# The second pass of a 192-row matmul as two 64-row tiles of the TensorE array

## Chip, cores, metric

The kernel runs on one core of one Trainium2 chip. The metric is the device time of a whole execution in microseconds (us). Ratios are the mean time of one kernel's fast runs over that of the other's of the same rounds, with a 95% interval; so they are not quite the ratio of the medians quoted beside them.

## The reference

```python
# x: (8, 4096, 192), weight_gen: (8, 4096, 8 heads, 7 taps)
w = softmax(weight_gen, axis=-1)
out = einsum('bshk,bskhg->bshg', w, windows_of_7_rows(x))   # dynamic convolution
h = out.reshape(32768, 192) @ w_in                          # 192 -> 2048
result = (h - tanh(h)) @ w_out                              # 2048 -> 192
```

## The kernel before

It works on 64 blocks of 512 tokens. POOL multiplies the seven shifted copies of x by the softmax weights (`prod`), DVE adds them in pairs (`gsum`), and PE transposes and sums the groups against an identity into `pc`. ScalarE (ACT) evicts `pc` into `convT` (input rows 0 to 127) and `convT1` (rows 128 to 191). Then PE makes `ph` = w_in x conv for two 128-wide f tiles at a time, ACT takes tanh (`th`), DVE subtracts (`gt`), and PE makes the output `po`. `pc`, `ph` and `po` lie in PSUM, where the kernel keeps the outputs of matmuls; to evict is to copy out of it. In the profiles, PEld is the loading of a matmul's weights.

192 input rows do not fill two passes of 128. The kernel before fills up with zeros: the columns 192 to 255 of each `gsum`, and the rows 64 to 127 of `w_in1`.

```python
    w_in1 = const.tile([P, F], BF16, name="w_in1")
    nc.vector.memzero(w_in1[D1:P, :])                            # D1 = 64, P = 128
    nc.gpsimd.dma_start(out=w_in1[0:D1, :], in_=moe_w_in[D0:D, :])
    # ... in the sums of a block:
                nc.gpsimd.memzero(acc[:, :, D:DP])               # L179: D = 192, DP = 256
    # ... in the first matmul; fa and fb are the two f tiles, ph has one PSUM bank for each:
            # L227 and L234: ph[a], ph[b] = w_in0 x convT        (128 rows)
            nc.tensor.matmul(ph[:, 0:TOK],                       # L241
                lhsT=w_in1[:, fa * P : (fa + 1) * P], rhs=convT1[:], start=False, stop=True)
            nc.tensor.matmul(ph[:, TOK : 2 * TOK],               # L248
                lhsT=w_in1[:, fb * P : (fb + 1) * P], rhs=convT1[:], start=False, stop=True)
    # ... (cut: loads, softmax, transposes L194 to L206, evictions, output L272 and L279)
```

The steps of transposing (`gen_phase_a2`), first matmul (`gen_phase_b`) and output matmul (`gen_phase_c`) of neighbouring blocks are interleaved in the program, and the compiler then orders the instructions of each engine.

The softmax here doesn't subtract the row's maximum and nothing guards it: scores larger than these inputs give would overflow.

## Time and profile before

1045.23 us, median of two runs. The table is from the windows view over eight blocks of the long stage (436.4 to 552.8 us) and from the busy table.

| engine | us busy per block | share of the whole span |
|---|---|---|
| PE | 14.2 | 89% |
| DVE | 11.8 | 77% |
| POOL | 11.4 | 71% |
| ACT | 10.3 | 64% |

The lines themselves, and how they are read, stand in the prediction. In short: a head of about 16 blocks, in which POOL and DVE lead, then 48 blocks in which PE sets the pace. A plain one of them takes 14.27 us. I split every run below at the end of block 15's last `gt`: the head is what comes before it, and the long stage is from there to block 63's last `gt`. Before, they took 341.4 and 691.9 us of a span of 1041.2, with 7.9 us of tail.

### The profile page before, as it was taken

The page shows a single profiled execution, that of the slowest core. Times are in us where ns is not written, and L with a number is a line of the kernel's source. Part 1 is how long each engine was busy: PE and PEld are TensorE (multiplying, and loading weights), DVE is VectorE, ACT ScalarE, POOL GpSimd, SP SyncE. Part 2 cuts the span into 40 slices and gives each one's busy share as a digit, 9 for nine tenths or more (in the row PEclk, how much of TensorE's full clock was granted, in tenths as well). Part 3 has the DMA queues.
Part 4 walks back from the last instruction along what each step waited for, and adds up shares of the span by engine and source line. Part 5 has one row for each costly group of instructions (what it writes and reads, how often), then busy time and mean ns, then how long its engine had stood idle before and what let it go on. Part 6 is the DMA issues. An engine that isn't in the chain of part 4 may idle for free.

```text
span 1041.2 us, 20956 instructions
## 1 busy us (share of the span) xinstructions
PE 931.3 (89%) x8192; PEld 661.6 (64%) x8192; DVE 803.0 (77%) x945; ACT 665.2 (64%) x961; POOL 739.3 (71%) x713
## 2 busy tenths in 40 slices
PE   0576777798999999999999999999999999999998
PEld 0344554465666777667776777667776777777776
DVE  1587777797887888788887888788887888877665
ACT  0254445465666777767776777677776777777775
POOL 4868868898786778867787778867787777882000
PEclk9999899899999999999999999999999999999999
DMA  8947588687997787777776777777876777510001
GB/s 167 314 132 230 169 242 250 202 264 223 331 289 208 236 242 222 220 214 235 238 219 205 236 237 233 216 211 231 243 223 202 235 227 239 153 62 27 21 31 47
DMA packets 306579, 211.48 MB, mean 203 GB/s; under 512 B 44312, under 2 KB 306288, under 8 KB 306480
## 3 DMA queue, kind: packets, MB, share of 16 engines
q1 hardware_dynamic: 304192, 208.58, 67.4%
q0 software_dynamic: 2288, 1.57, 1.1%
q8 instruction: 64, 1.05, 0.4%
q14 instruction: 35, 0.29, 0.1%
HBM read 186.52 MB, written 25.17 MB: 203 GB/s over the span
## 4 chain that ended last, share of the span: by engine, by line
PE 55%; POOL 17%; DVE 9%; issue 5%; ACT 5%; SPq 4%; DMA 3%; POOLq 0%; ACTq 0%; DVEq 0%
POOL prod L155 17%; PE po L272 10%; PE po L279 10%; PE ph L248 8%; PE ph L227 7%; PE ph L234 7%; PE ph L241 7%; DVE gt L258 5%; PE pc L194 2%; DVE gsum L174 2%; DMA wg_t<-in_weight_gen_dram 2%; SPq L123 2%; PE pc L206 2%; PE pc L198 2%; PE pc L202 2%
## 5 line engine op out<-in xcount | busy, mean ns | idle before, releaser
L155 POOL TENSOR_TENSOR prod<-xs,wsm 128x768 bf16<-128x768 f32 x448 | 687.1, 1563 | 100.1 <-DVE wsm L146 45.5
L256 ACT ACTIVATE th<-ph 128x1024 f32<-128x1024 f32 x512 | 519.1, 1023 | 283.9 <-PE ph L248 270.9
L258 DVE TENSOR_TENSOR gt<-ph,th 128x1024 bf16<-128x1024 f32 x512 | 609.9, 1210 | 83.0 <-ACT th L256 82.4
L272 PE MATMUL po<-w_out_t,gt 128*128 128x192 bf16 x2048 | 383.4, 248 | 2.1 <-ACT out_sb L288 2.1
L279 PE MATMUL po<-w_out_t,gt 128*128 128x192 bf16 x2048 | 383.1, 248 | 0.0
L227 PE MATMUL ph<-convT,w_in 128*128 128x512 bf16 x512 | 196.6, 384 | 57.0 <-DVE gt L258 55.5
L279 PEld LDWEIGHTS <-gt 128*128 128x128 bf16 x2048 | 201.8, 99 | 27.2 <-issue 4.8
L272 PEld LDWEIGHTS <-gt 128*128 128x128 bf16 x2048 | 201.9, 99 | 24.7 <-issue 1.3
L248 PE MATMUL ph<-convT,w_in 128*128 128x512 bf16 x512 | 197.1, 385 | 0.0
L241 PE MATMUL ph<-convT,w_in 128*128 128x512 bf16 x512 | 196.8, 384 | 0.0
L234 PE MATMUL ph<-convT,w_in 128*128 128x512 bf16 x512 | 196.6, 384 | 0.0
L174 DVE TENSOR_TENSOR gsum<-prod,prod 128x768 bf16<-128x768 bf16 x192 | 137.1, 759 | 41.1 <-POOL prod L155 41.1
L179 POOL MEMSET gsum<- 128x128 uint32 x192 | 38.6, 204 | 127.9 <-DVE gsum L174 126.5
L194 PE MATMUL pc<-ident,gsum 128*128 128x128 bf16 x384 | 84.9, 221 | 42.9 <-DVE gsum L174 32.1
L234 PEld LDWEIGHTS <-w_in 128*128 128x128 bf16 x512 | 50.4, 98 | 66.0 <-issue 65.8
L241 PEld LDWEIGHTS <-w_in 128*128 128x128 bf16 x512 | 50.5, 99 | 62.0 <-issue 3.0
L198 PE MATMUL pc<-ident,gsum 128*128 128x128 bf16 x384 | 84.9, 221 | 4.0 <-POOL gsum L179 3.9
L206 PE MATMUL pc<-ident,gsum 128*128 128x128 bf16 x384 | 85.1, 222 | 0.0
L248 PEld LDWEIGHTS <-w_in 128*128 128x128 bf16 x512 | 50.5, 99 | 54.4 <-issue 2.2
L202 PE MATMUL pc<-ident,gsum 128*128 128x128 bf16 x384 | 85.1, 222 | 0.0
L194 PEld LDWEIGHTS <-gsum 128*128 128x128 bf16 x384 | 38.0, 99 | 55.8 <-DVE gsum L174 33.2
L198 PEld LDWEIGHTS <-gsum 128*128 128x128 bf16 x384 | 37.8, 98 | 54.2 <-issue 26.3
(31 smaller groups left out, 579.6 us busy)
## 6 DMA issues: line engine op xcount, KB each, us to landing
xs<-in_x_dram SPq DMA_DIRECT2D x400, 384.0 KB
out_dram<-out_sb SPq DMA_DIRECT2D x64, 384.0 KB
xs<-in_x_dram SPq DMA_DIRECT2D x48, 288.0 KB
wg_t<-in_weight_gen_dram SPq DMA_DIRECT2D x64, 112.0 KB
w_out_t<-in_moe_w_out_dram POOLq DMA_DIRECT2D x1, 768.0 KB, 17.0
xs<-in_x_dram SPq DMA_DIRECT2D x8, 95.2 KB
xs<-in_x_dram SPq DMA_DIRECT2D x8, 94.5 KB
xs<-in_x_dram SPq DMA_DIRECT2D x8, 93.8 KB
```

What stands on the lines that cost most here:

```text
L155: nc.gpsimd.tensor_mul(prod[:, :, 0:D].rearrange("p j (h g) -> p j h g", h=H), xs[k][:].rearrange("p j (h g) -> p j h g", h=H), wsm[:, :, ...
L174: nc.vector.tensor_add(acc[:, :, 0:D], prods[taps[0]][:, :, 0:D], prods[taps[1]][:, :, 0:D])
L194: nc.tensor.matmul(pc[:, 0:P], lhsT=gsums[g][:, j0, 0:D0], rhs=ident[:], start=st0, stop=False,)
L198: nc.tensor.matmul(pc[:, P : 2 * P], lhsT=gsums[g][:, j1, 0:D0], rhs=ident[:], start=False, stop=False,)
L227: nc.tensor.matmul(ph[:, 0:TOK], lhsT=w_in0[:, fa * P : (fa + 1) * P], rhs=convT[:], start=True, stop=False,)
L234: nc.tensor.matmul(ph[:, TOK : 2 * TOK], lhsT=w_in0[:, fb * P : (fb + 1) * P], rhs=convT[:], start=True, stop=False,)
L241: nc.tensor.matmul(ph[:, 0:TOK], lhsT=w_in1[:, fa * P : (fa + 1) * P], rhs=convT1[:], start=False, stop=True,)
L248: nc.tensor.matmul(ph[:, TOK : 2 * TOK], lhsT=w_in1[:, fb * P : (fb + 1) * P], rhs=convT1[:], start=False, stop=True,)
L256: nc.scalar.activation(out=th[:], in_=ph[:], func=ACT.Tanh)
L258: nc.vector.tensor_sub(gt[:], ph[:], th[:])
L272: nc.tensor.matmul(po[:, 0:D], lhsT=gts[ft // 2][:, gto + j0 * P : gto + (j0 + 1) * P], rhs=w_out_t[:, ft, :], start=(ft == 0), stop=False,)
L279: nc.tensor.matmul(po[:, D : 2 * D], lhsT=gts[ft // 2][:, gto + j1 * P : gto + (j1 + 1) * P], rhs=w_out_t[:, ft, :], start=False, stop=(ft ...
```

## The change

It gives the second pass the 64 rows that it needs and is meant to run the passes of fa and fb at once, as two tiles: fa in rows 0 to 63 of the array, fb in rows 64 to 127. Going from full-array matmuls to these tiles, or back, is called a change of mode, or a switch, below. For that both halves of `w_in1` hold the same weights, and the last 64 columns of each `gsum` are copied behind themselves, so that `convT1` comes out with its 64 rows twice.

```diff
-    nc.vector.memzero(w_in1[D1:P, :])
     nc.gpsimd.dma_start(out=w_in1[0:D1, :], in_=moe_w_in[D0:D, :])
+    nc.gpsimd.dma_start(out=w_in1[D1:P, :], in_=moe_w_in[D0:D, :])
@@
-                nc.gpsimd.memzero(acc[:, :, D:DP])
+                nc.gpsimd.tensor_copy(acc[:, :, D:DP], acc[:, :, D0:D])
@@
-                lhsT=w_in1[:, fa * P : (fa + 1) * P],
-                rhs=convT1[:],
+                lhsT=w_in1[0:D1, fa * P : (fa + 1) * P],
+                rhs=convT1[0:D1, :],
@@
-                lhsT=w_in1[:, fb * P : (fb + 1) * P],
-                rhs=convT1[:],
+                lhsT=w_in1[D1:P, fb * P : (fb + 1) * P],
+                rhs=convT1[D1:P, :],
```

## The prediction

> **What bounds the kernel now.** I read the page first: the busy table, the 40 slices, the chain, the groups.
>
> ```profile
> PE 931.3 (89%) x8192; PEld 661.6 (64%) x8192; DVE 803.0 (77%) x945; ACT 665.2 (64%) x961; POOL 739.3 (71%) x713
> ...
> PE   0576777798999999999999999999999999999998
> ...
> PE 55%; POOL 17%; DVE 9%; issue 5%; ACT 5%; SPq 4%; DMA 3%; POOLq 0%; ACTq 0%; DVEq 0%
> ...
> L179 POOL MEMSET gsum<- 128x128 uint32 x192 | 38.6, 204 | 127.9 <-DVE gsum L174 126.5
> ```
>
> PE is at 9 tenths in all slices from the tenth on and at 5 to 8 before. So there are two stages: a head of some 290 us in which the chain runs through POOL's products and DVE's sums, and a long stage in which PE never stops. The memset row matters later: POOL already waits for DVE's gsum there.
>
> Next, the windows view over one stretch of the long stage, and the timeline of PE in it.
>
> ```profile
> 436.40:552.80 116.40, 113.75 (x1028) 81.65 (x1026) 94.30 (x118) 82.75 (x121) 91.21 (x89) 1.00 0.76 225
> ```
>
> ```profile
> 703.16 0.38 PE L227 MATMUL ph<-convT,w_in 128*128 128x512 bf16 x1
> 703.38 0.38 PE L234 MATMUL ph<-convT,w_in 128*128 128x512 bf16 x1
> 703.59 0.38 PE L241 MATMUL ph<-convT,w_in 128*128 128x512 bf16 x1
> 703.81 0.38 PE L248 MATMUL ph<-convT,w_in 128*128 128x512 bf16 x1
> 704.02 0.22 PE L194 MATMUL pc<-ident,gsum 128*128 128x128 bf16 x1
> 704.08 0.22 PE L198 MATMUL pc<-ident,gsum 128*128 128x128 bf16 x1
> ```
>
> The window holds 8 of the 64 blocks of 512 tokens: 14.55 us a block, of which PE is busy in 98%; DVE needs 94.30/8 = 11.8, POOL 11.4, ACT 10.3, and the DMA share 0.76 means some 11.1 at full use. The matmul records overlap, so I use the step from start to start: 0.216 us for a 512-column matmul (703.38 to 703.59), 0.055 for a 128-column one, and 0.0825 for a 192-column one (elsewhere in the same timeline). One block has 32, 32 and 64 of them: 6.91 + 1.78 + 5.28 = 13.97 us. That is nearly the whole period, so PE's start-to-start stream sets the long stage.
>
> One detail bears on the change. In time order, L241 is followed directly by L248 450 times out of 512; 61 times, about once a block, conversion matmuls stand between them:
>
> ```profile
> 707.31 0.38 PE L241 MATMUL ph<-convT,w_in 128*128 128x512 bf16 x1
> 707.82 0.22 PE L194 MATMUL pc<-ident,gsum 128*128 128x128 bf16 x1
> ...
> 708.04 0.38 PE L248 MATMUL ph<-convT,w_in 128*128 128x512 bf16 x1
> ```
>
> Such a pair cannot run side by side if the order stays as it is.
>
> **What the Trainium skill says.** "TensorE: Matmul & The Clock Gate", Part 3, says that tiles of different row groups run together, starting about 4 ns apart, and that a weight load overlaps a running matmul in that way only when the row group differs. "TensorEngine Tiling (Array Packing)", Key Properties: "Changing tiling mode (not just tile) drains the TensorE"; it gives no size for this. Its restrictions say that different row tiles must write to different PSUM banks; ph holds 2 x 512 fp32, and the halves go to the two tiles. "GPSIMD Engine Reference", section 4.1, calls one-input operations there roughly line-rate. The trace before agrees as far as it can: its 512-column step is 216 ns; but every record is a 128*128 operation, so neither the concurrency nor the drain is seen in it.
>
> **The change part by part.**
> *Removed.* Per pair of f tiles, two 216 ns passes become one. If the order stays, 450 pairs gain: 450 x 0.216 = 97 us of PE time; the 62 split ones gain nothing. The memset of w_in1 (one instruction, 0.9 us at the start) goes.
> *Added, PE.* Each pair is now a stretch in another tiling mode between full-array work: two switches, and four for a split pair, 450 x 2 + 62 x 4 = 1148 switches. Each costs an unknown s. Its bounds from the trace, as estimates: a matmul's record is 384 ns against a 216 ns step, so 168 ns lie between the end of streaming and the recorded end; and where a weight load and its matmul had both been waiting, the matmul starts 53 ns after the load at the least. If a switch waits for the whole record and then exposes the load, s is 168 + 53 = 221 ns. If only the array empties while reads go ahead, s is perhaps a third of the 168, with the load hidden: 56 ns. If it is overlapped, 0. Break-even is 97 / 1148 = 85 ns.
> I choose 60 ns as the middle: 1148 x 0.060 = 69 us added, 28 us net off PE.
> *Added, POOL.* 256 memsets of 204 ns become copies of 256 bf16 elements per partition. Near line rate with some dispatch I estimate 350 to 450 ns, so 256 x 0.2 = 50 us more busy time, 739 to some 790. In the long stage POOL has 14.55 - 11.4 = 3.1 us of slack a block and needs 0.8 of it: hidden. In the head POOL is on the chain: some 20 blocks' worth of products run there, but only two or so copies a block stand between one product and the next that the chain needs, so 20 x 2 x 0.2 = 8 us on the path. The wait for gsum is no new one.
> *Added, DMA.* w_in1's upper half is loaded a second time in the first tens of microseconds; the first matmul that needs it starts at about 38 us. Nothing.
> *Sum.* 51 to 52 of 64 blocks are in the long stage, so 0.8 of a change in PE's work reaches the end: 0.8 x (-28) = -23 us. With +8 of the head: -15. 1045 - 15 = 1030 us.
>
> **Rivals.**
> (a) The full drain. With s = 221, PE gains 97 and pays 254: +157, times 0.85 is +133, and 8 of the head, some 1185 us. For it: the page's bare word "drains", and the design before, which zero-pads 64 rows to 128 and pays 51 us of POOL memsets for that, as one would to stay in one mode. Against it: that padding also pays with a much smaller s.
> (b) A switch that costs almost nothing. PE's block falls from 14.3 to 12.8 us. Then the loop between POOL and DVE takes over: in one block POOL runs six products in a row (9.04 us), waits for DVE's sums, runs the four fills (now 0.4 each), the seventh product (1.54), and DVE's wsm (0.39) precedes the next. That is 9.04 + 0.8 + 1.6 + 1.54 + 0.39, with some 0.3 of handovers, 13.7 at worst with all fills on the path, 12.6 with one. So the gain ends near 1 us a block: 51 x 1.0 = 51 off, 8 back: about 1000 us. For it: the reported concurrency. Against it: the modes alternate 16 times a block, not in long runs.
> (c) Order. The compiler may place the matmuls otherwise; if more pairs are split, the gain shrinks and the switches grow. 62 more splits would cost 62 x 0.216 + 124 x 0.06 = 21 us of PE time. The trace before shows only the old order.
>
> **Range and chances.** I spread s as 0 to 30 ns (a quarter; 985 to 1008 us), 30 to 60 (a quarter; up to 1030), 60 to 110 (a fifth; up to 1075) and over 110 (three tenths; up to 1190). Two per cent are 21 us: faster below 1024, which is s under about 52 ns: 0.42. Within 2% up to 1066, s under about 100: 0.23. Slower: 0.35. The range that leaves a tenth on either side is 985 to 1150.
>
> **What would show it.** In the timeline the two 64-row matmuls of a pair should start within a few ns of each other; the step from the last full-array matmul to the first 64-row one, less 216 ns, is the first switch, and the step from the pair to the next full-array matmul, less 216, the second. My middle wants their sum near 120 ns. The sum over one fp is 3 x 216 + 120 = 768 ns, against 864 now. The copy's row should show 350 to 450 ns where the memset had 204. DVE and ACT should keep their busy times. The period of a block in the long stage should be near 13.9 us. I am wrong most surely if the pair does not overlap at all, or if the switch is as long as a matmul's recorded latency; and if POOL or DVE, not PE, fills the long stage, rival (b) has come.

## The result

The changed kernel took 1060.62 us, median of two runs (1059.72 and 1061.53), against 1045.23: ratio 1.0149, interval 1.0119 to 1.0178. The forecast was a gain of 15 us; there was a loss of 15.

The page of the changed kernel, answering to the busy table, the chain and the memset row of before:

```profile
PE 928.7 (88%) x8044; PEld 577.9 (55%) x8192; DVE 810.7 (77%) x944; ACT 664.2 (63%) x961; POOL 825.0 (78%) x714
...
PE 61%; POOL 19%; DVE 8%; SPq 4%; DMA 4%; issue 3%; ACT 1%; POOLq 0%; ACTq 0%
...
L241 PE MATMUL ph<-convT,w_in 64*128 64x512 bf16 x512 | 201.2, 393 | 22.8 <-issue 1.4
...
L248 PE MATMUL ph<-convT,w_in 64*128 64x512 bf16 x512 | 201.2, 393 | 0.0
L179 POOL COPY gsum<-gsum 128x256 bf16<-128x256 bf16 x192 | 105.9, 582 | 97.0 <-DVE gsum L174 96.3
...
L241 PEld LDWEIGHTS <-w_in 64*128 64x128 bf16 x512 | 47.4, 93 | 222.2 <-issue 222.2
```

PE's busy share has hardly moved, although a pair's two passes now run together: the busy time unites overlapping records, and a matmul's record is longer than its step, so it hides gaps. (148 matmul records are also missing from this trace.) Two new numbers stand out. A copy is recorded at 582 ns where the memset had 204. That is a mean of unlike cases: in the long stage, 50 copies beside which DVE ran only `gt` took 394 to 397 ns each, 41 beside `wsm` 616 to 619, and 82 beside the adds of `gsum` 713 to 1135 (median 726). And the weight load of L241 has 222 us of idle time before it, 434 ns for each of its 512: before, that load ran well ahead of its matmul.

The timeline of PE over one whole pair in the long stage (start, duration):

```profile
605.67 0.38 PE L227 MATMUL ph<-convT,w_in 128*128 128x512 bf16 x1
605.89 0.38 PE L234 MATMUL ph<-convT,w_in 128*128 128x512 bf16 x1
606.20 0.39 PE L241 MATMUL ph<-convT,w_in 64*128 64x512 bf16 x1
606.20 0.39 PE L248 MATMUL ph<-convT,w_in 64*128 64x512 bf16 x1
606.52 0.23 PE L194 MATMUL pc<-ident,prod 128*128 128x128 bf16 x1
606.59 0.22 PE L198 MATMUL pc<-ident,prod 128*128 128x128 bf16 x1
606.64 0.22 PE L202 MATMUL pc<-ident,prod 128*128 128x128 bf16 x1
```

The two tiles do start together. But the step from L234 to L241 is 0.31 us, not the 0.216 of a 512-column matmul, and the step from the pair to L194 is 0.32. Over the whole trace, in whole nanoseconds, the medians are:

| step, start to start | before | after | more than the 216 of one pass |
|---|---|---|---|
| L234 to L241 (into the tiles) | 216 | 312 | 96 |
| L241 to L248 (tile to tile) | 216 | 3 | |
| L248 to the next full-array matmul | 216 | 319 | 103 |
| that one to its follower (L194 to L198) | 56 | 66 | 10 more than before |

So the pair saves 213 ns, and the two changes of mode cost 96 + 103 + 10 = 209.

What fills these 96 and 103 ns, no record shows. The weight loads show only that nothing is loaded ahead across them. First before, then after:

```profile
703.38 0.10 PEld L241 LDWEIGHTS <-w_in 128*128 128x128 bf16 x1
703.59 0.10 PEld L248 LDWEIGHTS <-w_in 128*128 128x128 bf16 x1
703.81 0.10 PEld L194 LDWEIGHTS <-gsum 128*128 128x128 bf16 x1
```

```profile
605.67 0.10 PEld L234 LDWEIGHTS <-w_in 128*128 128x128 bf16 x1
606.20 0.09 PEld L241 LDWEIGHTS <-w_in 64*128 64x128 bf16 x1 [0.42 <-issue]
606.20 0.09 PEld L248 LDWEIGHTS <-w_in 64*128 64x128 bf16 x1
606.52 0.10 PEld L194 LDWEIGHTS <-prod 128*128 128x128 bf16 x1 [0.23 <-issue]
```

Before, L241's load starts at 703.38, when L234's matmul starts, one whole step ahead of its own matmul at 703.59. After, a load into another mode starts only 4 ns ahead of its matmul (median of all 512; the same 4 ns for the first load back in the full array).

In time, the long stage went from 691.9 to 699.3 us and the head from 341.4 to 350.8: 7.4 and 9.4 us in these two profiles. The profiled execution of the kernel before was a fast one (its span is 1041.2 us; one that took 1045.15 us in a later round has 1043.4), so the growth of a head, read against it, comes out some 2 us too large. The windows view over eight blocks of the long stage after:

```profile
450.00:567.90 117.90, 113.07 (x1009) 70.77 (x1026) 95.61 (x119) 82.55 (x121) 103.20 (x89) 1.00 0.75 223
```

Eight blocks take 117.9 us instead of 116.4. POOL has gone from 91.21 to 103.20 us of that and still has room; PE, which sets the pace, has none. A plain block has gone from 14.265 to 14.360 us.

### The profile page after: what moved, and what is told of

It reads as the page before. It is cut to its first block, busy times and chain, and to the rows that moved or that the text cites. A ratio compares the mean times of both kernels' runs of the same rounds, so it can differ in the third digit from the quotient of the medians.

```text
span 1057.9 us, 20805 instructions
## 1 busy us (share of the span) xinstructions
PE 928.7 (88%) x8044; PEld 577.9 (55%) x8192; DVE 810.7 (77%) x944; ACT 664.2 (63%) x961; POOL 825.0 (78%) x714
## 4 chain that ended last, share of the span: by engine, by line
PE 61%; POOL 19%; DVE 8%; SPq 4%; DMA 4%; issue 3%; ACT 1%; POOLq 0%; ACTq 0%
POOL prod L155 17%; PE po L272 13%; PE ph L241 12%; PE po L279 12%; PE ph L227 8%; PE ph L234 5%; PE pc L194 5%; DVE gt L258 4%; DMA wg_t<-in_weight_gen_dram 2%; PE pc L206 2%; PE pc L202 2%; PE pc L198 2%; SPq L123 2%; POOL gsum L179 2%; DVE gsum L174 2%
## 5 line engine op out<-in xcount | busy, mean ns | idle before, releaser
L227 PE MATMUL ph<-convT,w_in 128*128 128x512 bf16 x512 | 197.4, 386 | 58.6 <-DVE gt L258 56.1
L241 PE MATMUL ph<-convT,w_in 64*128 64x512 bf16 x512 | 201.2, 393 | 22.8 <-issue 1.4
L248 PE MATMUL ph<-convT,w_in 64*128 64x512 bf16 x512 | 201.2, 393 | 0.0
L179 POOL COPY gsum<-gsum 128x256 bf16<-128x256 bf16 x192 | 105.9, 582 | 97.0 <-DVE gsum L174 96.3
L174 DVE TENSOR_TENSOR gsum<-prod,prod 128x768 bf16<-128x768 bf16 x192 | 148.7, 808 | 38.6 <-POOL prod L155 38.5
L241 PEld LDWEIGHTS <-w_in 64*128 64x128 bf16 x512 | 47.4, 93 | 222.2 <-issue 222.2
L234 PE MATMUL ph<-convT,w_in 128*128 128x512 bf16 x364 | 140.9, 387 | 0.0
L194 PE MATMUL pc<-ident,gsum 128*128 128x128 bf16 x384 | 88.5, 230 | 37.3 <-DVE gsum L174 32.8
L202 PE MATMUL pc<-ident,gsum 128*128 128x128 bf16 x384 | 86.2, 224 | 4.7 <-POOL gsum L179 4.7
L234 PEld LDWEIGHTS <-w_in 128*128 128x128 bf16 x512 | 50.4, 98 | 67.7 <-issue 67.5
L194 PEld LDWEIGHTS <-gsum 128*128 128x128 bf16 x384 | 37.8, 98 | 90.5 <-issue 57.1
L198 PE MATMUL pc<-ident,gsum 128*128 128x128 bf16 x384 | 86.3, 225 | 0.0
L206 PE MATMUL pc<-ident,gsum 128*128 128x128 bf16 x384 | 86.2, 224 | 0.0
L132 ACT ACTIVATE e_t<-wg_t 128x224 f32<-128x224 f32 x64 | 24.9, 389 | 80.5 <-DMA wg_t<-in_weight_gen_dram 44.6
L146 DVE TENSOR_TENSOR wsm<-e_t,zr 128x224 f32<-128x224 f32 x64 | 27.1, 423 | 62.3 <-POOL prod L155 62.1
```

What stands on the lines that cost most here:

```text
L174: nc.vector.tensor_add(acc[:, :, 0:D], prods[taps[0]][:, :, 0:D], prods[taps[1]][:, :, 0:D])
L179: nc.gpsimd.tensor_copy(acc[:, :, D:DP], acc[:, :, D0:D])
L194: nc.tensor.matmul(pc[:, 0:P], lhsT=gsums[g][:, j0, 0:D0], rhs=ident[:], start=st0, stop=False,)
L227: nc.tensor.matmul(ph[:, 0:TOK], lhsT=w_in0[:, fa * P : (fa + 1) * P], rhs=convT[:], start=True, stop=False,)
L234: nc.tensor.matmul(ph[:, TOK : 2 * TOK], lhsT=w_in0[:, fb * P : (fb + 1) * P], rhs=convT[:], start=True, stop=False,)
L241: nc.tensor.matmul(ph[:, 0:TOK], lhsT=w_in1[0:D1, fa * P : (fa + 1) * P], rhs=convT1[0:D1, :], start=False, stop=True,)
```

## The experiments

**Theory A:** PE sets the long stage; each change of mode costs about 0.1 us and two of them eat the pass that a pair saves; POOL's longer copy costs something in the head. **Rival B:** PE's gain is real, but the slower copy and the loop of POOL and DVE hide it. **Rival C:** the tiles only start together and share the array's time. A later question, D, is what the head's 9.4 us are.

All runs, with their parts in us from the profiled execution (the median is that of the timed runs; a plain block is the mean of blocks 24 to 29, which lie between two batch boundaries):

| run | median | before | ratio (interval) | head | long stage | plain block |
|---|---|---|---|---|---|---|
| before | 1045.23 | | | 341.4 | 691.9 | 14.265 |
| after | 1060.62 | 1045.23 | 1.0149 (1.0119 to 1.0178) | 350.8 | 699.3 | 14.360 |
| e1 copy only | 1052.24 | 1045.68 | 1.0061 (1.0046 to 1.0076) | 346.8 | 695.1 | 14.265 |
| e2 tiles only | 1054.84 | 1045.68 | 1.0084 (1.0069 to 1.0099) | 348.4 | 696.0 | 14.358 |
| e3 half the switches | 1050.65 | 1045.68 | 1.0042 (1.0008 to 1.0076) | 349.8 | 692.0 | 14.100 |
| e4 one tile | 1126.55 | 1045.68 | 1.0771 (1.0750 to 1.0793) | 355.0 | 762.9 | 15.853 |
| e5 before, no fill | 1052.33 | 1044.70 | 1.0072 (1.0057 to 1.0087) | 352.5 | 690.7 | 14.265 |
| e6 after, no fill | 1058.23 | 1044.70 | 1.0127 (1.0112 to 1.0142) | 344.2 | 704.1 | 14.622 |
| e7 half, no fill | 1049.42 | 1044.70 | 1.0046 (1.0026 to 1.0066) | 351.0 | 690.2 | 14.063 |
| e8 half, spread | 1090.65 | 1044.70 | 1.0439 (1.0421 to 1.0456) | 349.7 | 731.8 | 15.343 |
| e9 free switch | 1002.10 | 1046.33 | 0.9580 (0.9559 to 0.9602) | 348.0 | 644.1 | 13.192 |
| e10 placebo | 1041.18 | 1046.33 | 0.9954 (0.9933 to 0.9975) | 339.6 | 691.9 | 14.265 |
| e11 after, dead write | 1060.07 | 1046.33 | 1.0125 (1.0099 to 1.0151) | 350.9 | 699.3 | 14.359 |
| e12 half, DVE evicts | 1101.61 | 1046.33 | 1.0527 (1.0498 to 1.0556) | 352.3 | 737.2 | 15.167 |
| e13 matmuls only | 1050.33 | 1045.97 | 1.0045 (1.0030 to 1.0060) | 347.1 | 696.0 | 14.358 |

### The two parts of the change by themselves: e1 and e2

e1 is the kernel before with POOL's copy in place of its memset; the copied columns meet zero weights, so the result is right.

```diff
-                nc.gpsimd.memzero(acc[:, :, D:DP])
+                nc.gpsimd.tensor_copy(acc[:, :, D:DP], acc[:, :, D0:D])
```

> The kernel before with one part of the change: POOL's fill is the copy (mirror of the last 64 columns) instead of the zero fill; the matmuls stay full 128-row passes against zero weight rows, so the result is right. Theory A (each change of tiling mode costs about 0.1 us on PE and two of them eat the pass that a pair saves; the longer fill costs only in the head): block period of the long stage stays 14.3 us, head some 9 us longer, total 1052 to 1056 us. Rival B (the slower fill and its wait for gsum hold back every block, and hide a real gain of PE): about 1060 us with a longer period, above 14.4.

e2 is the changed kernel with the memset put back (half of the result is wrong).

```diff
-                nc.gpsimd.tensor_copy(acc[:, :, D:DP], acc[:, :, D0:D])
+                nc.gpsimd.memzero(acc[:, :, D:DP])
```

> The changed kernel with the zero fill put back on POOL (rows 64 to 127 of the operands are then zero, so the result is wrong on purpose); both 64-row tiles and their mode switches stay. Theory A: the head goes back to that of before, the period stays 14.3 to 14.4 us, total 1048 to 1054 us. Rival B: the gain of PE comes out, period about 13 us, total under 1010 us.

The copy alone costs 0.61%, the tiles with the second load of `w_in1` 0.84% (e13, below, has the tiles without that load: 0.45%); together 1.45%, against 1.49% for the whole change. In the long stage they add up as well: 3.2 and 4.1 us, against 7.4. The plain block is 14.265 us with the copy and 14.358 with the tiles, so the copy is hidden there, as forecast, and the tiles make the block longer. Rival B falls: with the copy gone, no gain comes out. The copy's 3.2 us of the long stage lie at four batch boundaries (once in eight blocks, where DVE also clears the rows ahead of a sequence): blocks 22 and 23 took 31.6 us in e1 and 30.8 before. e2's head, which Theory A wanted back at 341, stayed at 348; that is question D.

### Do the tiles run side by side: e4

Both passes of a pair take the lower tile; two changes of mode a pair remain.

```diff
-                lhsT=w_in1[D1:P, fb * P : (fb + 1) * P],
-                rhs=convT1[D1:P, :],
+                lhsT=w_in1[0:D1, fb * P : (fb + 1) * P],
+                rhs=convT1[0:D1, :],
```

> The changed kernel with both 64-row matmuls of a pair in the same tile (rows 0 to 63), so they can't run side by side; same number of switches, right result. Theory A (the tiles really run side by side and save a pass of 0.216 us): step from L241 to L248 0.216 instead of 0.003 us, 452 x 0.213 = 96 us of PE more, total 1130 to 1150 us. Rival C (the two tiles only start together and share the array's time, the second switch hiding it): about 1060 us.

PE's timeline in e4:

```profile
611.54 0.38 PE L234 MATMUL ph<-convT,w_in 128*128 128x512 bf16 x1
611.85 0.39 PE L241 MATMUL ph<-convT,w_in 64*128 64x512 bf16 x1
612.08 0.38 PE L248 MATMUL ph<-convT,w_in 64*128 64x512 bf16 x1
612.38 0.23 PE L194 MATMUL pc<-ident,prod 128*128 128x128 bf16 x1
```

L241 to L248 is now 0.226 us, and the steps into and out of the mode are nearly what they were (312 and 309, against 312 and 319). The block is 15.85 us, 1.49 more, which is seven whole pairs at 213 ns. The total, 1126.55, lies a little below the range expected. So the tiles run side by side in full, and rival C falls. e4 also prices the changes of mode at the level of the whole kernel: it has as many passes as e1, the same copy and 1144 changes more, and is 74 us slower than e1.

### What a free switch would have given: e9

The kernel before, with the second pass cut to half its columns (wrong): PE saves 216 ns per pair, and no mode changes.

```diff
-                ph[:, 0:TOK],
+                ph[:, 0 : TOK // 2],
...
-                rhs=convT1[:],
+                rhs=convT1[:, 0 : TOK // 2],
```
(and the same for fb.)

> The kernel before with the second pass of each f tile cut to 256 of its 512 columns (wrong result on purpose): PE saves 0.216 us per pair of f tiles, as the two tiles would if changing the mode cost nothing, and nothing else changes. Theory A (PE sets the period of the long stage and the switches alone ate the gain): the period falls by over 1 us to 12.5 to 13.3 us, total 970 to 1005 us. Rival B (the loop of POOL and DVE is the true limit): period stays above 14 us, total above 1035 us.

1002.10 us, ratio 0.9580. The pass was worth having: PE was the bound, and the same saving without the switches is worth 4.2%, 44 of the 110 us that 512 pairs at 216 ns make. The block fell to 13.19 us, not to the 12.5 that PE alone would allow. The windows view over eight blocks of e9 shows what is next:

```profile
420.00:528.10 108.10, 102.00 (x1010) 82.06 (x1027) 101.48 (x119) 81.20 (x121) 90.33 (x89) 1.00 0.83 243
```

DVE is busy for 101.48 of 108.10 us, and PE, in which the waits for `gt` buffers were 85.7 us in this run against 55.5 before, no longer leads alone.

### Fewer switches: e3, e7 and two misses, e8 and e12

e3 takes two pairs of f tiles at a time and puts their four tile matmuls together; the program has 646 changes of mode instead of 1144. (Its edit is abridged here, as are those of e7 and e12.)

```diff
-        for fp in range(NFT // 2):          # full, full, tile, tile; tanh and subtract
+        for fp in range(0, NFT // 2, 2):    # two ph buffers, pairs 0 and 1
+            full(0, True)
+            tiles(0, False)
+            shrink(0)                        # tanh and subtract of pair 0
+            tiles(1, True)                   # pair 1 begins with its tiles
+            full(1, False)
+            shrink(1)
```

> The changed kernel with two pairs of f tiles issued together in the order full, full, four 64-row matmuls, full, full: by the program order, 646 changes of mode instead of 1144, the same matmuls otherwise. Theory A: 498 switches less at 0.10 us are 50 us of PE, of which 0.8 reach the end: 1015 to 1025 us, period near 13.6 us. Rival B: no change, 1058 to 1064 us.

e7 is e3 without POOL's fill: the transposing matmul takes the columns 64 to 191, so that the 64 rows wanted land in the upper half, and ACT evicts them twice.

```diff
-                lhsT=gsums[g][:, j0, D0:DP]
+                lhsT=gsums[g][:, j0, D - P : D]
@@
-            nc.scalar.activation(out=convT1[:, cols], in_=pc[:, 2 * P : 4 * P], func=ACT.Copy)
+            for r in (0, D1):
+                nc.scalar.activation(
+                    out=convT1[r : r + D1, cols], in_=pc[D1:P, 2 * P : 4 * P], func=ACT.Copy)
```

> Run e3 (two pairs of f tiles together, 648 switches) with run e6's eviction in place of POOL's copy. In e3 the period fell to 14.1 us only, while DVE's sums slowed beside the longer POOL work. Theory A: with that gone, 500 switches less give 0.7 us a block: period 13.5 to 13.9 us, total 1015 to 1035 us. If instead the three PSUM buffers, taken two at a time, hold PE back, it stays near 1045 us.

Both are faster than the changed kernel by 9 to 11 us and slower than the kernel before by under half a per cent. Fewer switches do shorten the block, to 14.10 and 14.06 us, but by less than half of what was expected. PE's timeline in e7 shows both sides:

```profile
601.60 0.22 PE L193 MATMUL pc<-ident,gsum 128*128 128x128 bf16 x1 [0.16 <-ACT convT L214]
601.65 0.22 PE L197 MATMUL pc<-ident,gsum 128*128 128x128 bf16 x1
601.71 0.22 PE L201 MATMUL pc<-ident,gsum 128*128 128x128 bf16 x1
601.76 0.22 PE L205 MATMUL pc<-ident,gsum 128*128 128x128 bf16 x1
601.91 0.60 PE L241 MATMUL ph<-convT,w_in 64*128 64x512 bf16 x4
602.45 0.60 PE L230 MATMUL ph<-convT,w_in 128*128 128x512 bf16 x2
```

Four tile matmuls with the change out take 0.54 us; two separate pairs with theirs would take 2 x 0.32, and a second change in. From the first pair of a stretch to the second the step is 222 to 224 ns, so inside a mode there is no such cost. But the line of L193 carries a wait for ACT's eviction of `pc`: in this block PE lost 326 ns there, and 154 and 86 ns at two other places, while one group of four was split 1 and 3 by the compiler's order. This settles the plain block: eight changes fewer than in the changed kernel are worth 8 x 104.5 = 836 ns by the table of steps, the three waits took 566 of that, and the block is 297 ns shorter. The plain blocks of e7 are also 0.20 us shorter than those of the kernel before, but each batch boundary costs 1.4 to 2.5 us more than there, and the head is 351.0 us.

e8 spread the second full pass of each two pairs into the next step, to hold fewer PSUM buffers at once:

```diff
             full(0, True)
             tiles(0, False)
-            shrink(0)
             tiles(1, True)
+            shrink(0)
+            yield
             full(1, False)
             shrink(1)
             yield
-            yield
```

> As e7, but only the first of the two f-tile pairs gets its second full-row pass at once; the other gets it in the next step, after output and conversion matmuls (640 switches). If the bunching of PSUM buffers holds e7 back, this one is 5 to 15 us faster than e7; if switches alone count, the two are equal within 4 us.

It held the second of each two buffers longer instead, from its first matmul to its `gt` 4.45 us (median in the long stage) where e7 has 3.80: 1090.65 us, with a block of 15.34. e12 moved the eviction of `convT` in e7 from ACT to DVE:

```diff
-            nc.scalar.activation(out=convT[:, cols], in_=pc[:, 0 : 2 * P], func=ACT.Copy)
+            nc.vector.tensor_copy(convT[:, cols], pc[:, 0 : 2 * P])
```

> Run e7 with the eviction of the full 128 rows of the conversion moved from ScalarE to VectorE. In e7, PE waited 0.33 and 0.26 us a block for ScalarE's evictions and so kept 14.1 us. If that wait is what holds e7's gain back, period 13.5 to 13.8 us and total 1018 to 1038 us; if VectorE becomes the limit, 1045 us or more.

1101.61 us. The first line of its waits says why: the eviction stood in DVE's queue (120 of its 128 follow a subtraction directly), and ACT's other half of it waited.

```profile
ACT convT L212 <- DVE convT L210: 227.6, 119, 7.0
```

### The fill removed: e5 and e6

e5 is the kernel before without any fill, by the trick of e7 (zero weight rows now in the lower half); e6 is the changed kernel with e7's eviction. e6 has both parts of the edit shown for e7; e5 has only the first, and the two halves of `w_in1` change places.

> The kernel before without POOL's fill: the transposing matmul takes the last 128 of the 192 columns, so that the 64 new ones land in the upper half, and the zero weight rows move to the lower half; result right, matmuls unchanged. It gives the price of the zero fill itself. Theory A (fill is off the path in the long stage): period 14.3 us, total 1035 to 1046 us, any gain from the head. Rival B (fill couples POOL and DVE in every block): below 1030 us.

> The changed kernel without POOL's copy: the upper half comes from the same 128-column trick and ScalarE evicts the 64 rows twice, once into each half; result right. In the program order 511 pairs stay whole (452 in the changed kernel), 1026 switches. Theory A: a pair saves 0.213 us and pays two switches of 0.096 and 0.113, so PE's period is again 14.0 to 14.4 us, and the copy's share of the loss (6 to 7 us) goes away: 1040 to 1056 us. Rival B: below 1025 us.

Both surprised me. e5 does less work and loses 7.6 us, all of it in the head (352.5); its long stage is 1.2 us shorter. e6 kept 511 of 512 pairs whole, yet its block grew to 14.62 us: it traded the copy, which had been hidden, for evictions on ACT, and in the block that I read PE waited 242 and 418 ns at two places that have no such gap before; there a block has one wait, of 295 ns. Neither supports rival B.

### The head: e10, e11, e13

e10 is the kernel before with one clearing moved at the start, which changes nothing but the compiled order of the first blocks. e11 is the changed kernel with the same clearing kept as a dead write.

```diff
-    nc.vector.memzero(w_in1[D1:P, :])
+    nc.gpsimd.memzero(w_in1[D1:P, :])
```

> The kernel before, its zeroing of w_in1 moved from DVE to POOL: same work on PE, ACT and in the loop, but the compiler's order of the first blocks differs. If the head's length hangs on that order and not on POOL's fill, the first 16 blocks end 3 to 12 us away from the 341 us of before, and the long stage is as before (692 us from block 16 to the end): 1040 to 1057 us. If the order doesn't matter: within 2 us of 1045.

```diff
     w_in1 = const.tile([P, F], BF16, name="w_in1")
+    nc.vector.memzero(w_in1[D1:P, :])
```

> The changed kernel with DVE's zeroing of w_in1's upper half kept (a dead write, overwritten by the load), so that DVE starts as in the kernel before: same work otherwise. If the head's loss comes from POOL's longer copy: 1058 to 1063 us, first 16 blocks again at 350 us. If from the order: the head moves by some us either way, total 1050 to 1064 us, long stage again 699 us.

e13 is the kernel before with nothing but the matmuls' row ranges changed; zero fill and zero weight rows stay (wrong). The compiled order was the same as before on every engine, instruction by instruction.

```diff
-                lhsT=w_in1[:, fa * P : (fa + 1) * P],
-                rhs=convT1[:],
+                lhsT=w_in1[0:D1, fa * P : (fa + 1) * P],
+                rhs=convT1[0:D1, :],
```
(and rows D1 to P for fb.)

> The kernel before with nothing changed but the two second-pass matmuls of a pair, which take rows 0 to 63 and 64 to 127 as two tiles (zero fill and zero weight rows stay, so half of the result is wrong on purpose). The compiled order is the same as before on every engine, instruction by instruction. If the head's loss of 7 us in e2 came from the tiles' switches, the first 16 blocks end again near 348 us; if from the second load of w_in1 and the order that came with it, near 341 us. The long stage: 696 us in both cases (period 14.36 us), so 1053 or 1048 us.

e13 is the cleanest measure of the tiles: ratio 1.0045, a plain block of 14.358 us, a long stage of 696.0. Its profiled run was the slowest of six (1052.76 against a median of 1050.33), so its head of 347.1 is some 2 us too long for the median. e2, which has the same matmuls but a second load of `w_in1` and another order, is 4.5 us slower by the medians. e10 and e5 show the head moving by -2 and +11 us in the profiles (-5 and +9 by the medians) when POOL's work is nearly the same or less. e11 shows that not every reordering moves it: 350.9.

For the copy there is a second witness. Followed along the chain up to the end of the head, POOL's fills stand on it for 3.6 us before, 12.7 us in e1 and 15.4 us after. That is more than the head grew, so part of it took the place of other work on the chain.

How much each part cost the head can be estimated from the ratios (times 1045 us), which rest on several runs each, less what the long stage of the profiles grew by (the long stage was the same to 0.1 us in before and e10, and in after and e11): the copy 6.4 - 3.2 = 3 us (e1); the tiles 4.7 - 4.1 = under 1 us (e13); the tiles with the second load of `w_in1` 8.8 - 4.1 = 5 us (e2), so some 4 us for that load and the order that came with it. Together that is 8 us, and the changed kernel has 15.6 - 7.4 = 8. Each is uncertain by 1.5 us or more. How the second load or its order does it was not traced. A rival for the head is untested, too: the clock granted to TensorE there (PEclk of the windows view) was 0.96 before and in e10, 0.94 after and in e13, 0.93 in e1 and e2. Whether that is a cause of a longer head or follows from its waits, no run separates.

## Why the prediction was wrong

- **What bounds the kernel:** right. e9 shows that a saving on PE reaches the end, though only 44 of 110 us of it, DVE being busy for 101.48 of 108.10 us by then, and e4 that added work does.
- **Concurrency:** right. The two tiles start 3 ns apart, and running them in one tile costs the whole pass again.
- **The saved passes:** right in size. 452 pairs stayed whole, 450 were forecast, and each saved 213 ns: 96 us.
- **The cost of a switch: this is the step that failed.** The prediction set s by choice: "I choose 60 ns as the middle: 1148 x 0.060 = 69 us added, 28 us net off PE." Measured are 96 ns in and 103 + 10 out, 104.5 on average, which lies above the break-even of 85 that the prediction had worked out. With it, 1144 x 0.1045 = 120 us against 96 saved. The argument for 56 ns had the weight load hidden; the trace shows no load ahead of a switch at all. The full drain of rival (a), 221 ns, was too high by a factor of two. Of the 30 us between forecast and result, this term with the split pairs makes about 27: -23 were forecast for PE, and the tiles cost the long stage 4.1 (e13).
- **Split pairs:** their number was right, their price not. Before, a split pair had a wait for `pc` of 295 ns between L241 and L194. After, the change out of the mode falls into that wait: the step is 319 ns where it was 511. So a split pair costs 4 x 104.5 - 295 = 123 ns, not 418. A block of seven whole pairs at -4 ns and one split at +123 comes to +95 ns; measured are 14.358 - 14.265 = +93 ns. This closes the account of the plain block.
- **POOL's copy:** hidden in a plain block, as forecast. The forecast of 350 to 450 ns fits the copies that DVE's adds and `wsm` left alone (394 to 397 ns in the long stage), not the rest. The prediction had no term for the batch boundaries (3.2 us). Its 8 us for the head agree with the estimate above by luck: the copy's share of that is about 3, and some 4 came with the second load of `w_in1`, for which the prediction had "Nothing".
- **Rival (b), the free switch at "about 1000 us":** confirmed by e9 at 1002.10, with the next limit close behind PE, as it said. Its 51 us off the long stage came as 48. That its 8 us for the head fitted is luck: e9 has no copy, and its head was 6.6 us longer in the profile all the same.
- **Slips in its working,** none of which moves the result much: PE's digits are 9 from the eleventh slice on, not the tenth, and 8 in the last. "53 ns after the load at the least" overlooks nine loads of the trace before that start 4 or 5 ns ahead of their matmul. Rival (a) multiplies by 0.85 where the sum has 0.8. And the trace before does not agree with the passage that a load overlaps a running matmul only in another row group: L241's load starts at 703.38 with L234's matmul, which uses the same 128 rows.
- **The range** was wide enough to hold 1060.62, and the chances gave "within 2%" only 0.23; the point was on the wrong side of zero.

No version with tiles beat the kernel before. The fastest correct run was e10 at 0.9954, which has nothing of the change in it.

## What to carry to other kernels

Before you split a pass into tiles, count the changes of mode that the program order will hold, not the passes saved: here a change cost 0.1 us, so a pair of 512-column passes between full-array work broke even at best. Bunching the tiles in one mode did shorten the plain block (14.06 us in e7), but bunching that holds more PSUM buffers at once can lose that again to waits for evictions; no version here won as a whole. And a change of under one per cent needs a run at the same compiled order beside it: moving one clearing in the first microsecond was worth as much as some of the effects in question.

## What the Trainium skill lacked or had wrong

- "TensorEngine Tiling (Array Packing)", Key Properties, says that a change of tiling mode drains the TensorE but gives no size. Here it cost 96 ns into two 64-row tiles, 103 ns back to the full array and 10 ns more on the second matmul after that; from pair to pair inside the mode the step was 222 to 224 ns, against 216 for full-array matmuls.
- No page that I read says what becomes of weight loads at a change of mode. Here the load of the first matmul after a change starts 4 ns before it, while without a change L241's load started 214 ns ahead (median).
- "TensorE: Matmul & The Clock Gate", Part 3, gives about 4 ns between the starts of concurrent tiles; 3 ns were measured, which agrees. Its measured speedups are for packed work; none is for tiles that alternate with full-array matmuls, where the same concurrency gave nothing (4 ns a pair).
- "GPSIMD Engine Reference", section 4.1, calls one-input operations roughly line-rate. In the long stage that is nearest for the copies that DVE's adds and `wsm` left alone: 395 ns for 256 bf16 elements per partition, 1.5 ns an element with all fixed costs. Beside `wsm` and the adds the same copy was recorded at 617 and 726 ns (medians); the zero fill of the same bytes took 204.
